# One matmul pass of an older attention head placed between the query projection and the scores, in the two groups that did not have it

## The chip, the cores and the metric

One core of a Trainium2 chip. The metric is the device time of the program in microseconds (us), as the median of several runs.

## The reference

Two branches share one layer norm of `x`; the result is `x + s * silu(...)`.

```python
xn = _layernorm(x)                                   # x: 1 x 2048 x 448
# attention: 16 query heads, 8 key/value heads, head size 256, the last 512 keys
q = (xn @ wq).reshape(B, Sq, Hq, Dh).transpose(0, 2, 1, 3)
scores = einsum("bhqd,bhkd->bhqk", q, k) * Dh ** -0.5
o = einsum("bhqk,bhkd->bhqd", softmax(scores), v)
s = o.transpose(0, 2, 1, 3).reshape(B, Sq, Hq * Dh) @ wo
# feed-forward
g = silu((gelu(xn @ w_gate) * (xn @ w_up)) @ w_down)
return x + s * g
```

All tensors are bf16.

## The kernel before

The kernel goes through 64 "heads" m: four blocks of 512 queries times 16 heads. The queries of 4, 6 or 8 heads are projected together, two heads ("a pair") at a time, on 64-row tiles of TensorE. Then come, for each head, eight score matmuls (full 128 rows), the exponentials, the division by their sum, a transpose by DMA, and, two heads later (`LAG`), eight matmuls with the values ("PV"). The group starts are m = 0, 4, 12, 18, 26, 34, 42, 50 and 58; the groups at 12 and 58 have six heads and a bank order of their own.

The kernel uses eight banks of PSUM, the memory that TensorE writes its products to, as four pairs: `cur` (two pairs, the banks AB of the scores) and `nxt` (two pairs, the banks BB of PV).

```python
groups = [0, Q0, Q0 + QS, Hq + 2] + list(range(Hq + 2 + QS, NQC * Hq, QS)) + [NQC * Hq]
...
for m in range(NS):
    split = m in groups and m not in (0, Q0, Hq + LAG)          # Q0 = 4, Hq + LAG = 18
    if m in groups:
        hi = groups[groups.index(m) + 1]
        three = hi - m == 6
        for i in range(m, hi, 2):                                 # the query pairs
            end = m > Hq and m % Hq == LAG
            p = (i - m) // 2
            q_group(i, ((cur, nxt[::-1], (cur[1], nxt[1])) if three else
                        (cur, nxt, (cur[0], nxt[0]), (cur[1], nxt[1])) if split else (cur, nxt) * 2)[p], end)
            ... # feed-forward gates after pairs of group m == Q0, ends of the block before, loads
    if split:
        pv(late[0], 0)                                            # the pass: first of the eight PV matmuls
    s_mm(m)                                                       # eight score matmuls, exponentials, transposes
    ...
    if len(late) == LAG:
        pv(late.pop(0), 1 if split else None)                     # the other seven, or all eight
    ... # output projection of a block ("burst") after its last head
    late.append(m)
```

`pv(m, 0)` is one 128x512 matmul (first half of the output columns, first key block); it opens the accumulation that `pv(m, 1)` goes on with.

```python
def pv(m, part=None):
    ...
    for e in range(2):
        b = BB[m % 2 * 2 + e]
        mms([... for j in range(NJ) if part is None or (part == 0) == (e == j == 0)], [b_va[g]] + b_pT[x], (b_ps[b],))
        if part == 0:
            break
        ... # eviction of the bank to SBUF
```

The softmax here doesn't subtract the row's maximum and nothing guards it: scores larger than these inputs give would overflow.

Of the kernel before, what the change touches and what calls it, by code (L numbers as in the profile page):

```python
# [168 lines left out]
def bass_recurrent_scan__sliding_block_cached__geglu_ffn__prompt_kernel(  # L169
# [15 lines left out]
    Hq = HD // Dh  # L185
# [19 lines left out]
    Q0 = 4  # L205
# [6 lines left out]
    with es:  # L212
# [158 lines left out]
        groups = [0, Q0, Q0 + QS, Hq + 2] + list(range(Hq + 2 + QS, NQC * Hq, QS)) + [NQC * Hq]  # L371
# [6 lines left out]
        def dma(q, o, i, reads=(), writes=(), after=()):  # L378
            K.op(q, lambda e, o=o, i=i: e.dma_start(o, i), reads, writes, dma=True, after=after)
# [192 lines left out]
        def sum_act(c, k, i=None):  # L572

            fs = {0: slice(0, 4), 1: slice(4, NH), None: slice(0, NH)}[i]
            o = lambda e, r: (actTh[:, c % 2, e * NH + fs.start:e * NH + fs.stop, r * HC:(r + 1) * HC],
                              b_actT[c % 2][e * NH + fs.start:e * NH + fs.stop])
            S = lambda j: (dn[c][0][j][0][:, fs, :], dn[c][0][j][1] if len(dn[c][0][j][1]) == 1 else dn[c][0][j][1][fs])
            j, (x, bx), (y, by), op = ((3, o(0, 0), o(0, 1), ALU.subtract), (2, o(1, 1), S(3), ALU.subtract),
                                       (0, S(2), o(0, 0), ALU.add), (1, o(1, 0), S(2), ALU.subtract))[k]
            add("dve", S(j)[0], x, y, bx + by, S(j)[1], op)  # L580
# [127 lines left out]
        def load_k(g):  # L708
            dma_t(kT[:, g, :, :], A_k_cache[0, g, Sk - W:Sk, :], (), (b_kT[g],))

        def load_v(g):
            dma("sp", va[:, g, :, :],
                A_v_cache[0, g, Sk - W:Sk, :].rearrange("(j p) d -> p j d", p=P), (), (b_va[g],))
# [88 lines left out]
        def q_group(n, pairs, more_act=False):  # L802

            c, h = divmod(n, Hq)
            units = [(b, lambda j, k, i=i: wq[:, k, (h + i) * Dh + j * P:(h + i) * Dh + (j + 1) * P],
                      wqr[:, h + i, :], slice(c * QC, (c + 1) * QC), b_wql[h // HG][:1], b_wql[h // HG][1:], b_xnT[c * 4:c * 4 + 4])
                     for i, b in enumerate(pairs)]
            group(units, 0, QC, True, True)
            for i, b in enumerate(pairs):
                s = qs(n + i)  # L810
                act(qT[:, s, 0, :], bank[b], ACT.Copy, (b_ps[b],), (b_qT[s][0],))
                if more_act and i:
                    act(qT[:, s, 1, :], bank[b + 1], ACT.Copy, (b_ps[b + 1],), (b_qT[s][1],))
                    continue
                K.op("dve", lambda v, s=s, b=b: v.tensor_copy(qT[:, s, 1, :], bank[b + 1]),  # L815
                     (b_ps[b + 1],), (b_qT[s][1],))

        AB, BB = [], []
        LAG = 2
# [44 lines left out]
        def load_g2(t, after=()):  # L864
            dma("pool", g2[:, t % NG2, :], g2d[t], (b_g2d[t],), (b_g2[t % NG2],), after)

        def burst_end(t, ns=(0, 1)):

            t4 = t % 4
            x, bx = (xr[:, t % NXR, :], b_xr[t % NXR]) if t < NT - 1 else (lastt[:, 2, :], b_lastt)  # L870
            g, bg = (g2[:, t % NG2, :], b_g2[t % NG2]) if t < NT - 2 else (lastt[:, t % 2, :], b_lastg[t % 2])
            cs = slice(ns[0] * N2, ns[-1] * N2 + N2)
            bx, by = [[b[n] for n in ns] for b in (bx, b_xs[t4])]
            add("dve", xs[:, t4, cs], xs[:, t4, cs], g[:, cs], by + [bg], by, ALU.mult)
            if t + NG2 < NT - 2:
                load_g2(t + NG2)
            add("dve", x[:, cs], xs[:, t4, cs], x[:, cs], by + bx, bx)
            dma("sp" if t >= NT - 4 else "pool", out_view[:, t, cs], x[:, cs], bx, ())
            if t + NXR < NT - 1:
                dma("pool", xr[:, t % NXR, :], x_view[:, t + NXR, :], (), b_xr[t % NXR])  # L880
# [117 lines left out]
        AB.extend(bk(cur, j) for j in range(4))  # L998
        BB.extend(bk(nxt, j) for j in range(4))
        for m in range(NS):  # L1000
            split = m in groups and m not in (0, Q0, Hq + LAG)
            if m in groups:
                hi = groups[groups.index(m) + 1]
                three = hi - m == 6
                for i in range(m, hi, 2):
                    end = m > Hq and m % Hq == LAG
                    p = (i - m) // 2
                    q_group(i, ((cur, nxt[::-1], (cur[1], nxt[1])) if three else (cur, nxt, (cur[0], nxt[0]), (cur[1], nxt[1])) if split else (cur, nxt) * 2)[p], end)
                    if m == 0:
                        sum_act(2, 2 + p)  # L1010
                    if m == Q0 and p == 0:
                        K.reuse(b_kT[2:6] + b_va[3:5])
                        for g in range(2, 6):
                            load_k(g)
                        for g in range(3, 5):
                            load_v(g)
                    if m == Q0 and p < 2:
                        gates3(2 * p)
                        gates3(2 * p + 1)
                    if m == Q0 + QS and p == 0:  # L1020
                        K.reuse(b_kT[6:] + b_va[5:] + [b for y in b_xr for b in y])
                        load_v(5)
                        for g in range(6, Hkv):
                            load_k(g)
                            load_v(g)
                        now = [[o for o in K.ops if o.eng == "pe"][-1]]
                        for t in range(NG2):
                            load_g2(t, now)
                        for t in range(NXR):
                            dma("pool", xr[:, t, :], x_view[:, t, :], (), b_xr[t], now)  # L1030
                    if end and p:
                        burst_end((m // Hq - 1) * 4 + p - 1)
                    if m > Hq and m % Hq == LAG + QS and p == 1:
                        burst_end((m // Hq - 1) * 4 + 3)
                if m == 0:
                    K.reuse([b for x in b_pT for b in x] + b_pn + b_p32)
            if m > Hq and m % Hq == LAG:
                K.reuse(b_pn + b_p32)
            if split:
                pv(late[0], 0)  # L1040
            s_mm(m)
            if m < LAG:
                if m == 0:
                    gates2 = down7(2, (BB[0], BB[1], AB[2], AB[3], BB[2], BB[3]), g2w, b_g2w, (3, 4, 6, 5, 2, 1),
                                   lambda: [sum_act(3, k) for k in range(4)])
                else:
                    gates3 = down7(3, (BB[1], BB[0], AB[2], AB[3], BB[2], BB[3]), g2w, b_g2w, (3, 4, 2, 5, 6, 1),
                                   lambda: [gates2(q) for q in range(4)])
                    K.reuse(b_pT[2])
                if m == LAG - 1:  # L1050
                    K.reuse(b_oT + [b for y in b_qT[:QS - Q0] for b in y])
                    assert not CASTS and not SUMS
            if len(late) == LAG:
                pv(late.pop(0), 1 if split else None)
            if m > Hq and m % Hq == LAG - 1:
                if m // Hq == 1:
                    for b in [y for x in b_xs for y in x]:
                        b.old.extend(y for t in range(4) for z in b_xnT[t] for y in z.readers + [z.writer])
                burst(m // Hq - 1)
            late.append(m)  # L1060
# [56 lines left out]
```

## Time and profile before

| | |
|---|---|
| time, median of the first 3 runs | 541.42 us (540.93 to 541.90) |
| span of the profiled run | 538.7 us |
| TensorE busy | 532.6 us (99%) |
| VectorE, ScalarE busy | 383.7 (71%), 314.4 us (58%) |

TensorE is the only engine near its limit. In the lines below, "PE" is a matmul and "PEld" a load of weights; a record's length isn't the time between two matmuls: records of 379 ns start 216 ns apart where 512 columns stream without a break (one "pitch"). Read starts, not lengths.

### The profile page before, as it was taken

The page shows a single profiled execution, that of the slowest core. Times are in us where ns is not written, and L with a number is a line of the kernel's source. Part 1 is how long each engine was busy: PE and PEld are TensorE (multiplying, and loading weights), DVE is VectorE, ACT ScalarE, POOL GpSimd, SP SyncE. Part 2 cuts the span into 40 slices and gives each one's busy share as a digit, 9 for nine tenths or more (in the row PEclk, how much of TensorE's full clock was granted, in tenths as well). Part 3 has the DMA queues.
Part 4 walks back from the last instruction along what each step waited for, and adds up shares of the span by engine and source line. Part 5 has one row for each costly group of instructions (what it writes and reads, how often), then busy time and mean ns, then how long its engine had stood idle before and what let it go on. Part 6 is the DMA issues. An engine that isn't in the chain of part 4 may idle for free.

```text
span 538.7 us, 10915 instructions
## 1 busy us (share of the span) xinstructions
PE 532.6 (99%) x4155; PEld 311.0 (58%) x4180; DVE 383.7 (71%) x839; ACT 314.4 (58%) x782; POOL 39.6 (7%) x78
## 2 busy tenths in 40 slices
PE   8999999999999999999999999999999999999998
PEld 5556656459644444984444469544444984444487
DVE  6689886799767757935765786367667944776785
ACT  5466354873668768116866850488488206876820
POOL 1131120000000010003001000120000003001010
PEclk9999999999999999999999999999999999999999
DMA  9568172932596796302861760067447302972721
GB/s 291 130 186 108 54 130 86 274 76 57 112 177 139 156 187 153 57 1 87 166 138 48 154 138 1 18 156 141 96 106 150 68 1 68 166 158 73 150 65 35
DMA packets 171605, 61.38 MB, mean 114 GB/s; under 512 B 155105, under 2 KB 168417, under 8 KB 171553
## 3 DMA queue, kind: packets, MB, share of 16 engines
q1 hardware_dynamic: 167488, 51.30, 44.7%
q0 software_dynamic: 3008, 8.72, 6.8%
q8 instruction: 33, 0.54, 0.4%
q10 hardware_dynamic: 1056, 0.66, 0.4%
q14 instruction: 20, 0.16, 0.1%
HBM read 19.76 MB, written 3.67 MB: 43 GB/s over the span
## 4 chain that ended last, share of the span: by engine, by line
PE 97%; DMA 1%; DVE 1%; ACT 0%; issue 0%
PE bank L394 97%; DMA pT<-pn 1%; DMA x<-in_A_x_dram 0%; ACT p L830 0%; DVE stats L441 0%; PE bank L492 0%; DVE pn L837 0%; ACT oTh L385 0%; DVE xn L467 0%; DVE mv L444 0%; PE bank L511 0%; DVE xnT L887 0%; DVE xnT L388 0%; DVE rden L834 0%; DVE rstd L461 0%
## 5 line engine op out<-in xcount | busy, mean ns | idle before, releaser
L830 ACT ACTIVATE p<-bank 128x512 f32<-128x512 f32 x256 | 150.6, 596 | 27.3 <-DVE pn L837 23.7
L394 PE MATMUL bank<-pT,va 128*128 128x512 bf16 x512 | 121.8, 379 | 0.1
L837 DVE TENSOR_SCALAR pn<-p,rden 128x512 bf16<-128x512 f32 x256 | 112.9, 483 | 10.0 <-DMA pT<-pn 4.9
L394 PE MATMUL bank<-kT,qT 128*128 128x512 bf16 x487 | 117.8, 379 | 1.7 <-ACT qT L385 0.3
L394 PE MATMUL bank<-xnT,wq 64*128 64x512 bf16 x768 | 94.9, 376 | 0.0
L394 PEld LDWEIGHTS bank<-pT,va 128*128 128x128 bf16 x512 | 49.9, 98 | 62.5 <-issue 2.5
L394 PEld LDWEIGHTS bank<-kT,qT 128*128 128x128 bf16 x512 | 49.8, 98 | 59.8 <-issue 0.8
L394 PE MATMUL bank<-xnT,wgu 64*128 64x512 bf16 (+2 forms) x768 | 84.0, 350 | 0.1
L385 ACT ACTIVATE qT<-bank 128x512 bf16<-128x512 f32 x76 | 44.1, 596 | 51.7 <-PE bank L394 50.0
L815 DVE CAST qT<-bank 128x512 bf16<-128x512 f32 x52 | 34.8, 690 | 48.9 <-PE bank L394 48.9
L394 PEld LDWEIGHTS bank<-xnT,wq 64*128 64x128 bf16 x768 | 36.7, 94 | 46.3 <-ACT p L830 1.7
L394 PEld LDWEIGHTS bank<-xnT,wgu 64*128 64x128 bf16 x768 | 37.6, 94 | 35.9 <-issue 0.4
L834 DVE RECIPROCAL rden<-rsum 128x2 f32<-128x2 f32 x128 | 21.2, 165 | 46.7 <-ACT p L830 46.3
L830 ACT ACTIVATION_READ_ACCUMULATOR p<-bank 128x1 f32 x256 | 51.6, 202 | 0.0
L394 PE MATMUL bank<-wt,sr 128*128 128x224 f16 x512 | 50.0, 259 | 0.0
L394 PEld LDWEIGHTS bank<-wt,sr 128*128 128x128 f16 x512 | 49.0, 98 | 0.4 <-ACT oTh L385 0.2
L385 ACT ACTIVATE gl<-bank 128x512 bf16<-128x512 f32 x56 | 33.0, 596 | 26.4 <-PE bank L394 22.1
L560 DVE TENSOR_TENSOR actTh<-bank,gl 128x512 f16<-128x512 f32 x56 | 37.4, 687 | 11.3 <-PE bank L394 5.8
L858 DVE TENSOR_SCALAR oTh<-bank 128x512 f16<-128x512 f32 x62 | 42.3, 683 | 0.0
L385 ACT ACTIVATE oTh<-bank 128x512 f16<-128x512 f32 x66 | 38.9, 590 | 4.1 <-PE bank L394 4.1
L394 PE MATMUL bank<-wt,oTh 128*128 128x224 f16 (+1 forms) x416 | 38.3, 252 | 0.0
L394 PEld LDWEIGHTS bank<-wt,oTh 128*128 128x128 f16 x416 | 37.2, 98 | 0.9
(77 smaller groups left out, 386.6 us busy)
## 6 DMA issues: line engine op xcount, KB each, us to landing
wtb<-in_A_wo_dram POOLq DMA_DIRECT2D x4, 896.0 KB, 10.7
wq<-in_A_wq_dram SPq DMA_DIRECT2D x2, 1536.0 KB, 8.9
va<-in_A_v_cache_dram SPq DMA_DIRECT2D x8, 256.0 KB, 6.5
pT<-pn SPq DMA_TRANSPOSE x128, 2.8
xr<-in_A_x_dram POOLq DMA_DIRECT2D x15, 112.0 KB, 2.3
wd<-in_B_w_down_dram SPq DMA_DIRECT2D x1, 1568.0 KB, 8.6
g<-g_all POOLq DMA_DIRECT2D x14, 112.0 KB, 2.3
out_dram<-xr POOLq DMA_DIRECT2D x12, 112.0 KB, 2.1
```

The costliest lines, as they stand in the source:

```text
L385: K.op("act", lambda e, o=o, i=i: e.activation(o, i, func, scale=scale), reads, writes)
L394: ins = e.matmul(o, lhsT=l, rhs=r, start=st, stop=sp, skip_group_check=True)
L560: K.op("dve", lambda e: e.tensor_tensor(actTh[:, c % 2, f, :], bank[b + 1], gl[:, s, :], ALU.mult), (b_ps[b + 1], b_gl[s]), (b_actT[c % 2] ...
L815: K.op("dve", lambda v, s=s, b=b: v.tensor_copy(qT[:, s, 1, :], bank[b + 1]), (b_ps[b + 1],), (b_qT[s][1],))
L830: K.op("act", lambda e, b=b, r=r, z=z: e.activation(p32[:, z, :], bank[b], ACT.Exp, scale=att_scale, accum_out=rsum[:, r:r + 1]), (b_ps[b] ...
L834: K.op("dve", lambda e, r=r: e.reciprocal(rden[:, r - 1:r + 1], rsum[:, r - 1:r + 1]), b_rsum[r - 1:r + 1], b_rden[r - 1:r + 1])
L837: K.op("dve", lambda e, r=r - 1 + t, z=(n - 1 + t) % NP32, y=y, t=t: e.tensor_scalar(pn[:, y, t, :], p32[:, z, :], rden[:, r:r + 1], None, ...
L858: K.op("dve", lambda v, i=i, b=b: v.tensor_scalar(oTh[:, i, :], bank[b], WS, None, op0=ALU.mult), (b_ps[b],), (b_oT[i],))
```

## The change

The second and the fourth group (m = 4 and m = 18) were excepted from the pass. The change lets them have it, so that all groups but the first do. The idea: when the last query matmul is done, there is a piece of work that TensorE can do before the scores.

```diff
-            split = m in groups and m not in (0, Q0, Hq + LAG)
+            split = m in groups and m > 0
```

It also gives these two groups the bank order that goes with the pass: the third and fourth query pairs take one pair of banks from each half.

## The prediction

> **What bounds the kernel now.** I read the page first, for the busy shares and for how many records each group has.
>
> ```profile
> PE 532.6 (99%) x4155; PEld 311.0 (58%) x4180; DVE 383.7 (71%) x839; ACT 314.4 (58%) x782; POOL 39.6 (7%) x78
> ...
> L394 PE MATMUL bank<-pT,va 128*128 128x512 bf16 x512 | 121.8, 379 | 0.1
> ...
> L394 PE MATMUL bank<-kT,qT 128*128 128x512 bf16 x487 | 117.8, 379 | 1.7 <-ACT qT L385 0.3
> L394 PEld LDWEIGHTS bank<-pT,va 128*128 128x128 bf16 x512 | 49.9, 98 | 62.5 <-issue 2.5
> L394 PEld LDWEIGHTS bank<-kT,qT 128*128 128x128 bf16 x512 | 49.8, 98 | 59.8 <-issue 0.8
> ```
>
> TensorE is busy for 532.6 of 538.7 us. A change that moves matmuls and removes none can gain only from TensorE's idle time. The score matmuls have 487 records for 512 weight loads, so 25 matmul records are missing; I return to these. Next, the chain of work that ended last, which shows where idle time sits at the query groups.
>
> ```profile
> 158.93 0.16 issue
> ...
> 250.31 0.16 issue
> 250.47 10.74 PE bank L394 x49
> ```
>
> Read at its face, the chain has TensorE stand for 0.16 us before the scores at 158.9 and at 250.3. These are the second and the fourth query group, the two that the diff changes. I then compared these joints with one that has the pass already, in the timeline. The second group (no pass):
>
> ```profile
> 158.85 1.41 PEld L394 LDWEIGHTS bank<-kT,qT 128*128 128x128 bf16 x8 [0.42 <-issue]
> 159.08 1.67 PE L394 MATMUL bank<-kT,qT 128*128 128x512 bf16 x7 [0.16 <-ACT qT L385]
> ```
>
> The third group (with the pass):
>
> ```profile
> 195.76 0.10 PEld L394 LDWEIGHTS bank<-pT,va 128*128 128x128 bf16 x1 [0.42 <-issue]
> 195.76 0.39 PE L394 MATMUL bank<-pT,va 128*128 128x512 bf16 x1
> 195.77 1.61 PEld L394 LDWEIGHTS bank<-kT,qT 128*128 128x128 bf16 x8
> 196.20 1.67 PE L394 MATMUL bank<-kT,qT 128*128 128x512 bf16 x7
> ```
>
> The reader is to see three things. The weight loads stand 0.42 us idle at both joints. At both joints there are eight loads of score weights and seven score matmuls, so the first score matmul has no record. And the hole that it leaves is the 0.16 us: in the second group its record would lie between 158.85 and 159.08. Last, I measured whole groups, from the first query matmul to the last PV matmul before the next group, with the engine busy times of given stretches (second group, fourth, sixth and eighth; queries, then heads).
>
> ```profile
> 146.35:158.55 12.20, 12.20 (x114) 5.33 (x112) 8.04 (x15) 6.55 (x14) 0.00 (x0) 1.00 1.04 179
> 158.55:186.28 27.73, 27.47 (x129) 12.45 (x128) 21.01 (x54) 24.42 (x73) 0.00 (x0) 1.00 0.71 150
> 237.86:249.94 12.08, 12.08 (x115) 5.38 (x113) 3.69 (x8) 5.82 (x11) 2.68 (x5) 1.00 0.12 37
> 249.94:277.67 27.73, 27.47 (x129) 12.42 (x128) 21.01 (x55) 24.76 (x74) 2.14 (x4) 1.00 0.72 155
> 339.18:351.26 12.08, 12.08 (x115) 5.38 (x113) 3.68 (x8) 5.83 (x11) 2.68 (x5) 1.00 0.12 35
> 351.26:379.29 28.03, 27.74 (x128) 12.38 (x128) 20.83 (x55) 24.59 (x73) 2.14 (x4) 1.00 0.71 148
> 440.81:452.88 12.07, 12.07 (x113) 5.37 (x113) 3.68 (x8) 5.82 (x11) 2.67 (x5) 1.00 0.12 36
> 452.88:480.61 27.73, 27.57 (x128) 12.40 (x128) 20.93 (x55) 24.86 (x74) 2.14 (x4) 1.00 0.74 155
> ```
>
> The first number after each stretch is its length. The eight heads take 27.73 us in the second and fourth group (no pass between), and 27.73 us in the eighth (pass between). This is the direct reading of what the change is worth. The sixth, at 28.03, has a stall of its own, treated under the rivals.
>
> **What the Trainium skill says.** "TensorE: Matmul & The Clock Gate", section "Back-to-back issue gap", gives a warm gap of N/2.4 + 2.5 ns, so 216 ns for 512 columns; the starts of successive score or PV matmuls in this trace are 216 ns apart. "TensorEngine Tiling (Array Packing)", section "Key Properties", says that a change of tiling mode drains the engine. The query projection runs on 64-row tiles and everything else on 128 rows, and the trace agrees: from the last query matmul to the next recorded full-row matmul it is 308 ns (195.453 to 195.761), 92 more than 216. The drain is owed once, whether a score or a PV pass comes next. "Perfetto Trace Analysis", section "Tensor Engine Instruction (MATMUL, LD_WEIGHTS)", says that a matmul's reported end is only estimated; here a record lasts 379 ns at a pitch of 216, so I count from start to start. "Runtime: NRT & Kernel Launch", section "Instruction fetch mechanics", says that programs are fetched in blocks of 16 KiB over a DMA queue of the sequencer; the page's 33 instruction packets of 0.54 MB are 16 KB each.
>
> **The change part by part.** Three things follow from the one condition, in two of nine query groups.
>
> 1. *The pass.* In each of the two groups one PV matmul of head m-2 (first half of the output columns, first key block) moves from behind eight score matmuls to before them: +216 ns before the scores, -216 ns after them. Work removed: 0. What could be gained is the idle time that it fills. Without it, the second score matmul starts 534 ns after the last query matmul (158.549 to 159.083); with it, 750 ns (195.453 to 196.203). The difference is 216, exactly the pass. Had it filled a hole of 160, the difference would have been 56. So: 2 x 0.00 us.
>
> 2. *The banks of the last two query pairs.* The third pair now takes one bank pair of each half, where it took both of the first half. Its second head reuses a bank pair that the second pair has just filled, after 4 x 216 = 0.86 us instead of some 3 us. In the fourth group ScalarE and VectorE have emptied it by 244.26 and 244.36, while the matmuls that want it come at about 244.77 (the third pair's start at 243.91 and 0.86; its load 0.21 earlier): free in time. In the second group the gate arithmetic of the feed-forward part is in the way:
>
> ```profile
> 152.26 0.62 DVE L615 SCALAR_TENSOR_TENSOR g<-th,cd 128x448 bf16<-128x448 f32 x1 [0.64 <-ACT th L385]
> 152.81 1.28 DVE L815 CAST qT<-bank 128x512 bf16<-128x512 f32 x2
> ```
>
> The first cast ends at 153.49. The weight load of the third pair's second head stands at 153.37 and its matmul at 153.58. With the new bank the load waits for that cast, to about 153.52 (an engine answered another's result after some 0.03 us, as in 151.620 to 151.654). Even with all of a load's 0.09 us exposed, the matmul starts by 153.62. Cost: 0.00 to 0.05 us, once. The eighth group shows that such a lateness hides: its weight loads once wait 0.30 us (at 465), yet its heads take 27.73 us like the others', since a load runs one pitch ahead of its matmul.
>
> 3. *Scores later.* The exponentials of head m and what follows come up to 0.22 us later in the second group; in the fourth not at all, since ScalarE's three query copies end at 251.44 and hold the first exponential anyway. Nothing of TensorE's waits for them: in the second group the last transposed probabilities land near 166.1 and are wanted near 167.5, estimates from the pitch of 216 ns and transposes of 2.7 us. The fourth group's last banks are evicted long before score tiles three and four, too. Cost: 0.
>
> Sum: 0.00 to +0.05 us of 541.4.
>
> **The rivals.** *The 0.16 us is real and the pass fills it.* For it: the chain says so, and only in the groups without the pass. Against: the seven records for eight loads, and 27.73 against 27.73. It would make 2 x 0.16 = 0.3 us, giving 541.1. *The pass upsets the transposes.* In the sixth and eighth group, both with the pass, weight loads wait 0.62 us (at 377.1) and 0.30 us (at 465) for transposed probabilities; the first makes the 28.03. Groups two and four have no such wait. If the pass causes it, the change brings up to 28.03 - 27.73 = 0.3 us twice, giving up to 542.0. Against: it comes seven and three heads after the pass, and instruction packets of 1.30 and 1.28 us lie at 374.1 and 461.6, just ahead of each. I hold these collisions to be chance; the change may shift them by a few tenths either way. *The reused banks stall every third pair of the second group harder than worked out*, say a whole load and drain: 0.2 us, giving 541.6. No rival reaches 1%.
>
> **The range and the chances.** The three runs of before span 540.93 to 541.90, so the median of a new set may differ by about 0.4 with no change at all. Adding a few tenths for moved collisions and the two rivals around a centre shift of zero, I predict 541.4 us, with 540.7 to 542.2 in 8 of 10 cases. 2% is 10.8 us, more than all of TensorE's idle time (6.1 us); a gain of it is impossible, and a loss of it would need a stall unlike any seen. Faster 0.003, same 0.992, slower 0.005.
>
> **What would show it right or wrong.** Right: at the second and fourth group a PV load precedes the score loads, the 0.42 us before it stays, the 0.16 us goes from the chain, and the groups still take 12.1 to 12.25 and 27.7 us. Step 2 shows as a short idle of the weight loads near 153.5. Wrong: a group's heads at 27.55 us or less (the hole was real), new waits for transposes in groups two and four alone (second rival), or query groups beyond 12.3 us.

## The result, and the profile after

| | before | after |
|---|---|---|
| median of 6 runs | 541.25 us (540.35 to 541.90) | 540.97 us (540.54 to 543.00) |
| span of the profiled run | 538.7 | 539.3 |

The ratio is 1.0001 (95% interval 0.9983 to 1.0019). The ratios aren't quite the ratios of the medians. The time is the same.

On each engine the order of the work is as intended: TensorE's differs in the two groups alone, and the other engines' not at all. The timeline of the second group after (start, length, engine, operation, and in brackets the idle time before it):

```profile
158.97 0.10 PEld L394 LDWEIGHTS bank<-pT,va 128*128 128x128 bf16 x1 [0.42 <-issue]
158.97 0.39 PE L394 MATMUL bank<-pT,va 128*128 128x512 bf16 x1
158.98 1.61 PEld L394 LDWEIGHTS bank<-kT,qT 128*128 128x128 bf16 x8
159.20 1.89 PE L394 MATMUL bank<-kT,qT 128*128 128x512 bf16 x8
```

The PV pass stands first, and the 0.42 us for which the weight loads are idle is unchanged. This time there are eight score matmuls for eight loads. The page's row of the score matmuls after says the same:

```profile
L394 PE MATMUL bank<-kT,qT 128*128 128x512 bf16 x512 | 121.0, 379 | 0.0
```

All 512 are recorded, with 0.0 us of idle ahead of them, where the first profile of the kernel before had 487 and 1.7 us. And the chain of work that ended last has no break at any query group until 453 us:

```profile
9.78 443.34 PE bank L394 x3464
```

The lengths of the groups after (second, fourth, eighth: queries, then heads; the first number after the stretch is its length):

```profile
146.47:158.66 12.19, 12.19 (x112) 5.32 (x112) 8.04 (x15) 6.54 (x14) 0.00 (x0) 1.00 0.90 184
158.66:186.43 27.77, 27.77 (x132) 12.37 (x128) 20.92 (x54) 24.59 (x73) 0.00 (x0) 1.00 0.72 149
238.01:250.09 12.08, 12.08 (x115) 5.38 (x113) 3.69 (x8) 5.82 (x11) 2.69 (x5) 1.00 0.12 35
250.09:277.82 27.73, 27.73 (x132) 12.43 (x128) 20.92 (x55) 24.76 (x74) 2.15 (x4) 1.00 0.74 155
...
452.73:481.07 28.34, 27.90 (x131) 12.35 (x128) 20.98 (x55) 24.85 (x74) 2.15 (x4) 1.00 0.71 152
```

The two changed groups take what they took: 12.19 and 27.77 against 12.20 and 27.73; 12.08 and 27.73 against the same. (The 0.04 us in the second is one load that comes late at 178.0 us.) The eighth group, in which nothing was changed, lost 0.61 us in this execution. Its timeline shows on what: the load for a PV pass waits for transposed probabilities.

```profile
462.28 0.76 PEld L394 LDWEIGHTS bank<-pT,va 128*128 128x128 bf16 x5 [0.93 <-DMA pT<-pn]
```

This alone is as much as the 0.6 us by which the profiled span after is longer than that of before. (The whole account: 0.1 us more at the start, 0.6 here, 0.2 at another late load at 509.7 us, and 0.3 less in the sixth group, where this time nothing was lost.) It is no effect of the two edited groups on themselves, but that it has nothing to do with the change had still to be tested.

### The profile page after: what moved, and what is told of

Its sections match the earlier page's. It is cut to its first block, busy times and chain, and to the rows that moved or that the text cites. A ratio compares the mean times of both kernels' runs of the same rounds, so it can differ in the third digit from the quotient of the medians.

```text
span 539.3 us, 10937 instructions
## 1 busy us (share of the span) xinstructions
PE 534.8 (99%) x4180; PEld 311.0 (58%) x4180; DVE 383.6 (71%) x839; ACT 314.7 (58%) x782; POOL 39.7 (7%) x78
## 4 chain that ended last, share of the span: by engine, by line
PE 97%; DMA 1%; DVE 1%; ACT 1%; issue 0%
PE bank L394 97%; DMA pT<-pn 1%; DMA x<-in_A_x_dram 0%; ACT p L830 0%; DVE pn L837 0%; DVE stats L441 0%; ACT qT L385 0%; PE bank L492 0%; DVE xn L467 0%; DVE mv L444 0%; DVE rden L834 0%; PE bank L511 0%; DVE xnT L887 0%; DVE xnT L388 0%; DVE rstd L461 0%
## 5 line engine op out<-in xcount | busy, mean ns | idle before, releaser
L394 PE MATMUL bank<-kT,qT 128*128 128x512 bf16 x512 | 121.0, 379 | 0.0
```

The costliest lines, as they stand in the source:

```text
L394: ins = e.matmul(o, lhsT=l, rhs=r, start=st, stop=sp, skip_group_check=True)
```

## The experiments

My theory: the pass only changes the order of TensorE's work, so it can neither gain nor lose, whether in two groups or in all. Rivals: the 0.16 us that the first profile shows before the scores is real idle time, which the pass fills; the pass makes transposes late; or the new banks cost something. Eight runs were made, two of them repeats, all with a correct result. The first four ran on one chip, where the kernel before had a median of 540.96 us (11 runs), the last four on another, where it had 540.64 us (7 runs).

Two figures are taken from every profile below. Where I give the length of a stretch without showing its row, it is counted from the first weight load of its phase to the first of the next, as this doesn't depend on missing matmul records. "Late" is by how much the first load of a PV pass comes over one pitch (216 ns) after the load before it; counted are the 62 PV passes of a profile that follow scores. An "instruction packet" is a DMA packet that brings a block of the program (a "fetch").

### The kernel before, once more

No edit.

> The kernel before, once more, for its profile. If the waits for transposed probabilities are chance collisions with program fetches, this profile has them in other heads than the first profile of the same program (there: near 377.1 and 465 us), again 2.4 to 3.5 us after an instruction packet, and the span differs by a few tenths of a us. If they belong to the program (to the pass in the sixth and eighth group), they are in the same heads with the same lengths. On the missing records: if the 0.16 us before the scores of the second and fourth group is a hole in the records, another profile of the same program can have all 512 score records and no such idle; if it is idle time, it is there again.

It had 540.45 us and a span of 538.6. Its timeline at the second group, and its row of score matmuls:

```profile
158.96 0.33 PEld L394 LDWEIGHTS bank<-kT,qT 128*128 128x128 bf16 x3 [0.42 <-issue]
158.97 0.60 PE L394 MATMUL bank<-kT,qT 128*128 128x512 bf16 x2
```

```profile
L394 PE MATMUL bank<-kT,qT 128*128 128x512 bf16 x512 | 121.0, 379 | 0.0
```

The same program, without the pass, now has all 512 records, and the first score matmul starts 0.01 us after its load. The 0.16 us was a hole in the records, not idle time. In the first profile the holes came evenly: the chain has runs of 49 matmuls and then a break, and where such a break falls inside a run of score matmuls, the starts stand 431 to 432 ns apart, two pitches, while the loads stay at 216. The late PV loads were in other places: at 174.6, 306.0 and 360.4 us, where the first profile of this program had them at 377.8 and 465.3. One of the three is in the second group, which has no pass here. So it takes no pass for a load to be late.

### The pass taken out of all groups

Against the kernel before; the condition also governs the bank order, so that goes as well:

```diff
-            split = m in groups and m not in (0, Q0, Hq + LAG)
+            split = False
```

> The pass is taken out of all groups, six more than in the kernel before. Theory (the pass is only a change of order): heads of an undisturbed eight-head group still take 27.73 us, and the time stays within 0.1% of before, 541.3. Rival (the pass fills a real hole of 0.16 us a group): 6 x 0.16 = 1.0 us more, 542.3 us, and heads of some 27.9 us.

541.31 us; ratio to before 0.9998 (0.9980 to 1.0016). The fourth and the eighth group:

```profile
238.83:251.02 12.19, 12.19 (x113) 5.37 (x113) 3.99 (x8) 6.13 (x11) 2.68 (x5) 1.00 0.14 46
251.02:278.75 27.73, 27.73 (x130) 12.42 (x128) 20.75 (x56) 24.72 (x75) 2.21 (x4) 1.00 0.73 151
442.24:454.43 12.19, 12.19 (x113) 5.37 (x112) 3.98 (x8) 6.12 (x11) 2.67 (x5) 1.00 0.14 43
454.43:482.17 27.74, 27.74 (x131) 12.46 (x130) 20.86 (x56) 24.73 (x75) 2.14 (x4) 1.00 0.69 152
```

The eighth group had the pass and lost it, and takes 27.74 us as against 27.73. The rival's 1.0 us isn't there, and 27.9 us in an undisturbed group even less. The interval alone, +-0.18% or 1 us, could hardly have decided it; the stretches do. The profile's span was 539.9 us, 1.2 us over the first profile of before. 0.7 of it was lost in the first 8.8 us, where both programs are the same and wait for the first rows' layer norm; the rest is five late PV loads against two. So the pass is worth nothing in the six groups that had it, either.

### The pass, without the banks that go with it

Against the kernel after:

```diff
-  ... if three else (cur, nxt, (cur[0], nxt[0]), (cur[1], nxt[1])) if split else (cur, nxt) * 2)[p], end)
+  ... if three else (cur, nxt) * 2)[p], end)
```

> The kernel after, but with the query pairs on the banks as they were where no pass stands, so that the pass goes into a bank that the last query pair has just filled. Theory: ScalarE evicts that bank 0.37 us after the last query matmul's start, the pass would start at 0.31, so it waits about 0.09 us in each of the six eight-head groups: 0.5 us in all, 541.8. Rival 1 (a load runs ahead and hides it): 0.0. Rival 2 (a whole eviction of 0.6 us is waited for): 3.6 us, 544.9.

542.02 us; ratio 1.0014 (0.9996 to 1.0032), which does not settle it by itself. The timeline of the second group does:

```profile
159.01 0.10 PEld L394 LDWEIGHTS bank<-pT,va 128*128 128x128 bf16 x1 [0.54 <-ACT qT L385]
```

The load stands 0.54 us idle where it is 0.42 in the kernel after, and it now waits for ScalarE's copy of a query bank. All six eight-head query stretches take 12.31 us where the kernel after has 12.19: 0.12 each, 0.7 us in all, a little over the 0.09 and 0.5 expected. Rival 1 and rival 2 fall. It says what the bank order is for: the pass is free only with it.

### The banks, without the pass

Against the kernel after:

```diff
-            if split:
-                pv(late[0], 0)
             s_mm(m)
 ...
-                pv(late.pop(0), 1 if split else None)
+                pv(late.pop(0), None)
```

> The kernel after, but only the new banks of the last two query pairs, and no pass. Theory: 0.0 us, 541.3; the weight load of the third pair's second head in the second group waits for VectorE near 153.6 by some 0.15 us, its matmul by 0.00 to 0.05. Rival (the reused banks stall a pair by a load and drain): 0.2 us in the second group, a query stretch of 12.4 us instead of 12.2.

541.22 us; ratio 1.0000 (0.9979 to 1.0020). The loads of the second group's third pair, in the timeline:

```profile
153.20 0.10 PEld L394 LDWEIGHTS bank<-xnT,wqr 64*128 64x128 bf16 x2
153.59 0.35 PEld L394 LDWEIGHTS bank<-xnT,wq 64*128 64x128 bf16 x6 [0.29 <-DVE qT L815]
```

The load comes 0.17 us late, waiting for VectorE's cast, and the query stretch is 12.19 us as ever. The lateness is there and costs nothing.

### The kernel after, once more

No edit.

> The kernel after, once more, for its profile. Chance collisions: the waits of weight loads for transposed probabilities are in other heads or of other lengths than in the first profile of it (177.5, 305.4, 359.9, 461.2, 509.1 us), each 2.4 to 3.5 us after an instruction packet. The pass as the cause: waits in the second and fourth group again, in the same heads.

540.33 us, span 538.5, the shortest of all the profiles. Its late PV loads come at 360.3, 417.5, 461.7 and 465.0 us, where the first profile of after had 178.0, 305.8, 360.3, 462.3 and 509.7. None is in the second or fourth group. The 0.82 us at 462.3 has become 0.19 at 461.7 and 0.12 at 465.0. So the longer span of the first profile after was no effect of the change. "Other places" holds only in part, though: the loads near 360.3 and near 462 us belong to the same two heads in both profiles, with other lengths. The two profiles of the kernel before share none. The spans of the two programs, 538.7 and 538.6 against 539.3 and 538.5, overlap.

### TensorE's program shifted against its fetches

Against the kernel after, waits that are met already are issued twice in TensorE's first 130 operations:

```diff
-                    eng.wait_ge(self.sem[d.eng], d.val)
+                    for i in range(1 + PAD * (name == "pe" and o.idx < 130)):    # PAD = 1
+                        eng.wait_ge(self.sem[d.eng], d.val)
```

> The kernel after with about a hundred waits that are already met, doubled in TensorE's program before its 130th operation, so that every later fetch of its program comes some 10 us of work earlier. If the late transposes come from fetches, they move with the instruction packets and still lie 2.4 to 3.5 us after one. If they come from the pass, they stay in their heads. Time within 0.2% of after.

543.9 us, span 542.1, 118 instructions more. My 0.2% was a miss: the feed-forward phase before 60 us took 3.3 us longer (1.3 by 14.4 us, another 2.0 at one wait for VectorE's sums at 54.5 us); from there on the shift is constant. I didn't look for the reason. What it was for came out as expected in two of three late loads: packets of 16 KB now lie at 363.5 and 407.3 us, other places of the program than the 370.8, 417.6 and 461.6 us of the second profile of after, and 3.7 and 3.4 us behind them the PV loads at 367.2 and 410.8 us are late, in heads that are late in no other profile. The third, at 363.6 us, decides nothing: it is the load near 360 us again, moved by 3.3 us like the whole program, and so is the packet of 8 KB that lies 3.0 us ahead of it.

Over all ten profiles, 37 PV loads were late by more than 0.08 us. They are not spread at random: they fall on 15 of the 62 heads, and the load near 360 us is late in seven of the ten profiles, in those of the two kernels without any pass too. The DMA packet records have an instruction packet 2.7 to 4.4 us ahead of 36 of them, and of only 90 of the 583 that weren't late. (The range is read off these same loads; the 2.4 to 3.5 us of the expectations were counted from the load before.) That the fetch delays a transpose is thus well supported, but no run removed a fetch, so I do not call it shown. That the pass does not cause it is shown: late loads come in the second group with the pass (178.0 us) and without it (174.6 us, twice), the kernel with no pass at all has five of them, no fewer than any other, and which heads are hit, and by how much, differs between two profiles of one program.

### A useless full-row matmul between the query pairs, and beside the scores

Both against the kernel after; 23 extra matmuls of 128x512 in each. One argument is put in words.

```diff
+        def dummy(b):
+            mms([(bank[b], ident[:, :], kT[:, 0, 0, :], True, True)], [b_ident, b_kT[0]], (b_ps[b],))
 ...  # the first kernel: ahead of each query pair but a group's first
+                    if p:
+                        dummy(first bank of this pair)
 ...  # the second kernel: ahead of a group's first scores, as many
+            if m in groups:
+                for i in range(m + 2, hi, 2):
+                    dummy(AB[0])
             s_mm(m)
```

> The kernel after with one useless full-row 128x512 matmul ahead of every query pair but a group's first, into the bank that this pair overwrites: 23 in all. The result stays right. Theory (each change between 64-row tiles and full rows is paid, 92 ns in and 95 ns back, beside the 216 of the pass): 23 x 0.40 = 9.3 us, ratio 1.017. Rival (the change of tiling is hidden by loads that run ahead): 23 x 0.216 = 5.0 us, 1.009.

> The kernel after with the same 23 useless full-row matmuls, but all of a group's ahead of the group's first scores, beside other full-row matmuls. Theory: no change of tiling is added, so 23 x 0.216 = 5.0 us, ratio 1.009. If it takes as long as the other placing, the changes of tiling cost nothing.

Between the pairs: 551.43 us, ratio 1.0196 (1.0179 to 1.0213). Beside the scores: 546.77 us, ratio 1.0113 (1.0098 to 1.0128). The eighth group, first with the matmuls between the query pairs, then with them beside the scores:

```profile
449.61:463.09 13.48, 13.48 (x116) 5.41 (x115) 3.98 (x8) 6.12 (x11) 2.68 (x5) 1.00 0.14 43
463.09:490.82 27.73, 27.73 (x130) 12.46 (x128) 20.82 (x56) 24.75 (x75) 2.35 (x4) 1.00 0.66 150
```

```profile
445.77:457.96 12.19, 12.19 (x113) 5.37 (x112) 3.99 (x8) 6.12 (x11) 2.68 (x5) 1.00 0.13 41
457.96:486.34 28.38, 28.38 (x133) 12.72 (x131) 20.88 (x56) 24.98 (x75) 2.14 (x4) 1.00 0.68 145
```

Three matmuls cost 13.48 - 12.19 = 1.29 us, 0.43 each, among the queries, and 28.38 - 27.73 = 0.65 us, 0.22 each, among the scores. The difference, 0.21 us, is the change from 64-row tiles to full rows and back (0.19 was expected). Times 23 this makes 9.9 and 5.0 us; the medians are 10.8 and 6.1 us above that of before, so about 1 us more in both. That is about the size of what the late PV loads cost in these two profiles (late by 0.23 to 0.78 us and 0.16 to 0.68 us, of which some 1.2 and 1.1 us in all exceed 0.2 us each). So the joint between queries and heads costs the change of tiling and no more, whatever full-row matmul comes next. The starts say the same directly: in all groups but the first, the next full-row matmul starts 308 or 309 ns after the last query matmul, whether it is a score matmul (second profile of before), a PV pass (kernel after) or a useless one (this run). Only the pass on the old banks has more, some 423 ns in the six eight-head groups. The 0.42 us for which the loads stand idle there isn't time that a pass can fill.

## Why the prediction was right

The number alone proves little: 540.97 us lies among the medians that the kernel before itself had (540.64 to 541.25). The steps were right as follows.

- *No gain from the 0.16 us (step 1).* Right: in both changed groups the second score matmul moved back by one pass and the heads took the same time. The second profile of before settles what had been inferred from seven records for eight loads, and the kernel without any pass gives the same with six more groups. One of the prediction's signs was empty, though: the 0.16 us did go from the chain, but it is gone from the second profile of before as well, which has no pass.
- *The reused banks (step 2).* Right in kind and in cost. The second group's late load, in the timeline of after:

```profile
153.65 0.36 PEld L394 LDWEIGHTS bank<-xnT,wq 64*128 64x128 bf16 x6 [0.29 <-DVE qT L815]
```

  In the time of the profile before (0.11 us less) that is 153.54; I had said 153.52. The matmul started at 153.70, one pitch after the one before it: the cost is 0.00 of the 0.00 to 0.05. The fourth group has no such wait.
- *Scores later (step 3).* Right: in the second group the first exponential starts 1.17 us after the last query matmul, where it was 0.95; in the fourth 1.39 both times. Nothing waited for it.
- *Late transposes as chance (second rival).* Right in that the pass isn't the cause. "Chance" is too simple: the same few heads are hit again and again, and only which of them, and how hard, changes. The link to instruction packets, seen on two cases then, held in 36 of 37.
- *A change of tiling is paid once.* Right, and 0.21 us there and back. ("Everything else on 128 rows" holds from the heads on; the gate and up projections of the feed-forward part run on 64-row tiles as well.)
- *The late load that hides.* Confirmed and sharpened: a stretch grows by what its load is late beyond about 0.2 us. Late by 0.12, 0.18 and 0.18 us: +0.00; by 0.30: +0.10; by 0.51: +0.31; by 0.82: +0.62.
- *TensorE's idle time of 6.1 us.* Too large, though the argument from it (no gain of 2%) only gets stronger: the missing records count as idle. With all records the same kernel is busy for 534.8 of 538.6 us, 3.8 us idle.

The size that I had clearly off is in an expectation, not in the prediction: the padded program's 3.3 us.

## What to carry to other kernels

Where TensorE is busy without a break, a change of order is worth what idle time it fills, and one should make sure that this idle time exists: count weight loads against matmul records, and compare whole stretches between joints of either kind, before believing a small gap. When two kernels differ by 0.1% in one profile each, take a second profile of each before looking for a cause. A bank order that lets work in is itself needed: the pass alone, without it, costs 0.12 us a group.

## What the Trainium skill lacked or had wrong

- "TensorE: Matmul & The Clock Gate", section "Back-to-back issue gap", gives some 131 ns for N = 512 in a stream of loads and matmuls, and calls 216 the gap of the isolated case. In these profiles a stream with one load per 128x512 matmul runs at 216 ns.
- "TensorEngine Tiling (Array Packing)", section "Key Properties", says that a change of tiling mode drains the engine, without a size. Here a change from 64-row tiles to full rows and back costs 0.21 us.
- No page that I read says by how much a weight load may come late at no cost: here up to about 0.2 us, one pitch, with 512 columns.
- No page that I read warns that a profile's matmul records may be missing at even distances (25 of 512 score matmuls in one of two profiles of the same program, none in the other), and that a false idle time of 0.16 us then stands in the chain of waits.
- No page that I read ties instruction packets to late transfers: 36 of 37 late loads here had one 2.7 to 4.4 us ahead, against 90 of 583 others, and one of them cost 0.6 us.
